# Softmax probabilities of ten units multiplied by their reciprocal on VectorE instead of GpSimd

## Chip, cores and metric

One core of a Trainium2 chip runs the whole program. The metric is the device time of one launch in microseconds (us); lower is better. The kernel before took 682.22 us (median of three runs, 682.05 to 683.24).

## What is computed

Causal attention over 4 batches, 12 heads, 448 positions and 64 columns a head, then a gated feed-forward layer on the 1792 resulting rows of 768 columns:

```python
scores = scale * np.matmul(q, k.transpose(0, 1, 3, 2))
scores = np.where(mask, -1000000000.0, scores)
attn = np.exp(scores - np.max(scores, axis=-1, keepdims=True))
attn = attn / (np.sum(attn, axis=-1, keepdims=True) + 1e-09)
attn_out = np.matmul(attn, v)
# rows x of 768 columns from attn_out, then
xn = x / np.sqrt(np.mean(x * x, axis=-1, keepdims=True) + 1e-06) * rms_g
g = xn @ w_gate
out = ((g * (1.0 / (1.0 + np.exp(-g)))) * (xn @ w_val)) @ w_out
```

The change touches one line of this: the division of `attn` by its row sums.

## The kernel before

Attention is done in **units**: two heads (`e` = 0 and 1) times a stretch of queries of one batch. The units come in three groups. The first group is units 0 to 11 (`ENDS[0]` is 12), each of 256 queries and 256 keys; its scores are held as a block of 128 queries by 128 keys and one of 128 by 256, for each of the two heads. So one step over the scores of a unit is four instructions: 128x128, 128x256, 128x128, 128x256.

What happens to one unit, engine by engine:

- TensorE makes the scores `s_ps` (line 193).
- VectorE adds the mask, scales, writes them to SBUF as `sp` and takes the row extremes `nm` (line 202, four instructions, each with a short accumulator read).
- ScalarE takes the exponential in place, with the row sums `sm` (line 205), and adds the tiny constant (line 227).
- VectorE takes the reciprocal `rs` of the four sums (`norm`, line 214).
- The probabilities `sp` are multiplied by `rs`: on GpSimd for units 0 to 9 (line 210), on ScalarE for units 10 and 11 (line 208).
- TensorE transposes `sp` into `t_ps` (head 0) and `x_ps` (head 1) (line 249). ScalarE copies the first and VectorE the second into `pt` (lines 255 and 253).
- TensorE multiplies `pt` by the values into `a_ps` (line 275), and VectorE copies that to `xr` (line 292).

Six buffers of `sp` serve three units at a time, and two banks hold `s_ps`.

The program writes every engine's order out by hand: `round_steps` gives a round of six ticks per unit, and `post(delay, fn)` puts a step some ticks later. Every engine then works through its own list in that order, and waits by semaphores alone. In the first group a round of unit p makes the scores of unit p + 3, the products of unit p, and the transposes of unit p + 1. Between these steps other work is threaded: weights are unpacked by one ScalarE step (line 414), one GpSimd step that flushes tiny values in place (line 415) and two VectorE steps (lines 417 and 419), and split into a high and a low part (lines 429 and 431); `xr` is split likewise (lines 335 and 336) and squared (GpSimd, line 103) and summed (VectorE, line 318); and the first feed-forward products run (lines 475 to 477). The GpSimd queue in this stretch holds the multiplications of line 210, the flushes of line 415 and the squares of line 103, one after the other.

After the first group the second group (products on ScalarE at line 208) and the third run threaded into the feed-forward products, and the feed-forward layer of the last rows ends the program.

Of the kernel before, what the change touches and what calls it, by code (L numbers as in the profile page):

```python
# [39 lines left out]
ENDS = [max(i for i, u in enumerate(UNITS) if u[0] == g) + 1 for g in range(NG)]  # L40
# [22 lines left out]
def attention_ffn(ctx: ExitStack, tc: tile.TileContext, qk0, qk1, qk2, v, v2, w, g, out, out2):  # L63
# [7 lines left out]
    nc = tc.nc  # L71
# [22 lines left out]
    def bank(tag, bufs=1):  # L94


        return ps.tile([P, W], F32, tag=tag, name=tag + "_ps", bufs=bufs)
# [34 lines left out]
    def post(delay, fn):  # L132
        if delay <= 0:
            fn()
        else:
            later.setdefault(now[0] + delay, []).append(fn)
# [14 lines left out]
    def load_qk(p):  # L151
        if p < len(UNITS):
            _, kind, _, _, row, _ = UNITS[p]
            raw_qk[p] = raw.tile([P, 2, W], F32, tag="qk", name="qk_r")
            if kind == 2:
                nc.sync.dma_start(out=raw_qk[p], in_=qk2[row])
            else:
                nc.sync.dma_start(out=raw_qk[p][:, 0], in_=(qk0, qk1)[kind][row])
# [10 lines left out]
    def blocks(kind):  # L169

        return [(0, P), (P, 2 * P)] if kind == 0 else [(0, KEYS[kind])]

    def steps_s(p):


        if not 0 <= p < len(UNITS):
            return []
        _, kind, _, _, _, _ = UNITS[p]
        pr = hs[p] = dict(norms=[])
        bl = blocks(kind)  # L180
        nb = 2 * len(bl)

        def scores(pss):
            for i, (o, wd) in enumerate(bl):
                for h in range(1 + (kind == 2)):
                    for e in range(2):
                        r = raw_qk[p][e * D: (e + 1) * D, h]
                        if kind == 2:
                            ps, q0, nq = pss[e][h * D: (h + 1) * D, :wd], 0, D
                        else:  # L190
                            ps, q0, nq = pss[e][:, o: o + wd], i * P, P
                        k0 = nq if kind else 2 * P
                        nc.tensor.matmul(ps, r[:, q0: q0 + nq], r[:, k0: k0 + wd],  # L193
                                         start=True, stop=True)

        def softmax(e, i, pss):
            o, wd = bl[i]
            ps, sp = pss[e][:, o: o + wd], pr["sp"][e][:, o: o + wd]
            n = len(bl) * e + i
            nm, sm, rs = (pr[m][:, n: n + 1] for m in ("nm", "sm", "rs"))  # L200
            mk = mask2 if kind == 2 else mask[:, 3 * P - wd:]
            nc.vector.tensor_tensor_reduce(  # L202
                out=sp, in0=ps, in1=mk, scale=nsc, scalar=3.0e38,
                op0=ALU.add, op1=ALU.min, accum_out=nm)
            post(T["exp" if p >= ENDS[0] else "exp0"], lambda: nc.scalar.activation(  # L205
                sp, sp, AF.Exp, bias=nm, scale=-1.0, accum_out=sm))
            if ENDS[0] - 2 <= p < ENDS[1]:
                pr["norms"].append(lambda: nc.scalar.mul(sp, sp, rs))
            else:
                pr["norms"].append(lambda: nc.gpsimd.tensor_scalar(  # L210
                    sp, sp, rs, 1.0, op0=ALU.mult, op1=ALU.mult))

        def norm():
            nc.vector.reciprocal(pr["rs"][:, :nb], pr["sm"][:, :nb])  # L214
            post(2 if ENDS[0] - 2 <= p < ENDS[0] else 0, lambda: [f() for f in pr["norms"]])

        def step():
            for nm in ("nm", "sm", "rs"):
                pr[nm] = st_p.tile([P, 4], F32, tag=nm, name=nm)
            pr["sp"] = [sp_p.tile([P, S], F32, tag="sp", name="sp") for _ in range(2)]  # L220
            pss = [bank(t_) for t_ in "xy"] if p > ENDS[1] + DP and p % 2 == 0 else [
                bank("s", 2) for _ in range(2)]
            scores(pss)
            for e in range(2):
                for i in range(len(bl)):
                    softmax(e, i, pss)
            post(T["exp" if p >= ENDS[0] else "exp0"], lambda: nc.scalar.activation(
                pr["sm"][:, :nb], pr["sm"][:, :nb], AF.Identity, bias=tiny))
            post(T["norm1" if kind else "norm0"], norm)
            post(2, lambda: load_qk(p + 4))  # L230

        return [step]
# [602 lines left out]
    with tc.manual_schedule():  # L835
# [157 lines left out]
        for q in range(21):  # L993
            i, p = divmod(q, 3)
# [58 lines left out]
```

## Time and profile before

| what | value |
|---|---|
| median of three runs | 682.22 us (682.05 to 683.24) |
| profiled execution | 681.84 us, its span 680.0 us |
| TensorE matmul busy | 667.7 us, 98% of the span |
| VectorE busy | 535.2 us, 79% |
| ScalarE busy | 378.3 us, 56% |
| GpSimd busy | 287.7 us, 42% |
| granted TensorE clock | full in every slice of the span |

The shares are means over a program of different stages. The first sixty microseconds hold the first group of units, and only they contain instructions that the change moves. In rows of the trace a line shows start and duration in us; consecutive VectorE instructions overlap at their ends, so what one of them costs the next is the distance between starts, not the duration.

### The profile page before, as it was taken

The page shows a single profiled execution, that of the slowest core. Times are in us where ns is not written, and L with a number is a line of the kernel's source. Part 1 is how long each engine was busy: PE and PEld are TensorE (multiplying, and loading weights), DVE is VectorE, ACT ScalarE, POOL GpSimd, SP SyncE. Part 2 cuts the span into 40 slices and gives each one's busy share as a digit, 9 for nine tenths or more (in the row PEclk, how much of TensorE's full clock was granted, in tenths as well). Part 3 has the DMA queues.
Part 4 walks back from the last instruction along what each step waited for, and adds up shares of the span by engine and source line. Part 5 has one row for each costly group of instructions (what it writes and reads, how often), then busy time and mean ns, then how long its engine had stood idle before and what let it go on. Part 6 is the DMA issues. An engine that isn't in the chain of part 4 may idle for free.

```text
span 680.0 us, 11926 instructions
## 1 busy us (share of the span) xinstructions
PE 667.7 (98%) x4116; PEld 550.8 (81%) x4116; DVE 535.2 (79%) x1059; ACT 378.3 (56%) x855; POOL 287.7 (42%) x262
## 2 busy tenths in 40 slices
PE   8989999999999999999999999999999999999997
PEld 5566877777777767777777777888999999999997
DVE  4998998999888486877777878487577866889982
ACT  6986779787876444545545353434534343355540
POOL 4971121222235427565765665563333342402220
PEclk9999999999999999999999999999999999999999
DMA  8765788787977556777667645316775457563541
GB/s 269 243 235 189 230 244 291 230 262 242 283 260 283 164 159 233 216 242 207 228 213 239 208 159 182 122 62 197 250 242 178 161 194 240 196 172 89 155 140 59
DMA packets 71356, 138.81 MB, mean 204 GB/s; under 512 B 7744, under 2 KB 39232, under 8 KB 71296
## 3 DMA queue, kind: packets, MB, share of 16 engines
q1 hardware_dynamic: 71296, 138.05, 63.0%
q8 instruction: 33, 0.54, 0.3%
q14 instruction: 27, 0.22, 0.1%
HBM read 104.21 MB, written 33.82 MB: 203 GB/s over the span
## 4 chain that ended last, share of the span: by engine, by line
PE 68%; DVE 1%; ACT 1%; DMA 0%; issue 0%; SPq 0%; DVEq 0%; ACTq 0%
PE s_ps L625 10%; PE m_ps L475 9%; PE m_ps L625 9%; PE m_ps L477 9%; PE m_ps L476 9%; PE y_ps L625 5%; PE a_ps L275 5%; PE x_ps L625 4%; PE t_ps L249 4%; PE s_ps L193 2%; PE x_ps L193 2%; DVE w_r L450 1%; DMA w_o<-wsum 0%; ACT sp L205 0%; ACT w_c L414 0%
## 5 line engine op out<-in xcount | busy, mean ns | idle before, releaser
L475 PE MATMUL m_ps<-xh,w_h 128*128 128x512 f32 x276 | 117.3, 425 | 0.0
L210 POOL TENSOR_SCALAR sp<-sp,rs 128x384 f32<-128x384 f32 (+2 forms) x112 | 77.7, 711 | 90.7 <-DVE rs L214 86.1
L205 ACT ACTIVATE sp<-sp,nm 128x384 f32<-128x384 f32 (+3 forms) x168 | 87.1, 521 | 41.3 <-DVE nm L202 41.3
L477 PE MATMUL m_ps<-xh,w_l 128*128 128x512 f32 x276 | 108.4, 393 | 0.0
L476 PE MATMUL m_ps<-xl,w_h 128*128 128x512 f32 x276 | 108.3, 392 | 0.0
L415 POOL TENSOR_SCALAR w<-w 128x768 f32<-128x768 f32 x36 | 39.8, 1108 | 104.4 <-ACT w_c L414 98.3
L103 POOL TENSOR_TENSOR a_l<-w_q,a_h 128x768 fp32r<-128x768 f32 x24 | 48.2, 2007 | 81.0 <-ACT a_h L516 81.0
L275 PEld LDWEIGHTS a_ps<-pt,v_r 128*64 128x64 f32 (+1 forms) x864 | 42.1, 137 | 31.9 <-issue 9.7
L275 PE MATMUL a_ps<-pt,v_r 128*64 128x128 f32 (+2 forms) x864 | 58.5, 268 | 6.0 <-DVE pt L253 3.2
L103 POOL TENSOR_TENSOR w_l<-w_r,w_h 128x768 fp32r<-128x768 f32 x30 | 59.5, 1992 | 6.2 <-ACT w_h L429 6.0
L475 PEld LDWEIGHTS m_ps<-xh,w_h 128*128 128x128 f32 x276 | 51.9, 188 | 11.8 <-issue 3.7
L477 PEld LDWEIGHTS m_ps<-xh,w_l 128*128 128x128 f32 x276 | 51.9, 188 | 11.8
L253 DVE COPY pt<-t_ps 128x384 f32<-128x384 f32 (+1 forms) x71 | 42.4, 597 | 23.9 <-PE t_ps L249 23.5
L475 PE MATMUL m_ps<-hh,w_h 128*128 128x512 f32 x144 | 58.6, 407 | 0.0
L202 DVE CUSTOM_DVE_ANT_0 sp<-s_ps,mask 128x128 f32<-128x128 f32 (+3 forms) x136 | 49.7, 414 | 10.9 <-PE s_ps L193 9.9
L476 PEld LDWEIGHTS m_ps<-xl,w_h 128*128 128x128 f32 x276 | 52.2, 189 | 7.6
L477 PE MATMUL m_ps<-hh,w_l 128*128 128x512 f32 x144 | 56.3, 391 | 0.0
L476 PE MATMUL m_ps<-hl,w_h 128*128 128x512 f32 x144 | 56.2, 390 | 0.0
L249 PE MATMUL t_ps<-ident,sp 128*128 128x128 f32 (+1 forms) x309 | 50.1, 275 | 0.1
L249 PEld LDWEIGHTS t_ps<-ident,sp 128*128 128x128 f32 (+1 forms) x309 | 37.9, 138 | 14.3 <-issue 2.0
L193 PE MATMUL s_ps<-qk_r 64*128 64x128 f32 (+3 forms) x296 | 42.6, 425 | 0.5 <-DVE nm L202 0.4
L516 ACT CAST a_h<-w_q 128x768 fp32r<-128x768 f32 (+1 forms) x48 | 35.0, 754 | 14.1 <-DMA w_q<-wz 4.3
(194 smaller groups left out, 1667.9 us busy)
## 6 DMA issues: line engine op xcount, KB each, us to landing
w<-in_w SPq DMA_DIRECT2D x36, 768.0 KB, 5.7
w<-w_c SPq DMA_DIRECT2D x36, 384.0 KB, 5.8
w_r<-w SPq DMA_DIRECT2D x36, 384.0 KB, 4.5
qk_r<-in_qk SPq DMA_DIRECT2D x48, 256.0 KB, 4.6
qk_r<-in_qk SPq DMA_DIRECT2D x12, 512.0 KB, 5.7
v_r<-in_v SPq DMA_DIRECT2D x12, 448.0 KB, 4.8
v_r<-in_v SPq DMA_DIRECT2D x24, 192.0 KB, 3.0
wy<-w_r SPq DMA_DIRECT2D x24, 192.0 KB, 4.3
```

The costliest lines, as they stand in the source:

```text
L103: nc.gpsimd.tensor_tensor(out_, a, b, op=op)
L193: nc.tensor.matmul(ps, r[:, q0: q0 + nq], r[:, k0: k0 + wd], start=True, stop=True)
L202: nc.vector.tensor_tensor_reduce(out=sp, in0=ps, in1=mk, scale=nsc, scalar=3.0e38, op0=ALU.add, op1=ALU.min, accum_out=nm)
L205: post(T["exp" if p >= ENDS[0] else "exp0"], lambda: nc.scalar.activation(sp, sp, AF.Exp, bias=nm, scale=-1.0, accum_out=sm))
L210: pr["norms"].append(lambda: nc.gpsimd.tensor_scalar(sp, sp, rs, 1.0, op0=ALU.mult, op1=ALU.mult))
L249: nc.tensor.transpose(ps[:kb, at: at + P], pr["sp"][e][:, o + kb * j: o + kb * (j + 1)], ident)
L253: nc.vector.tensor_copy(pt[:kb, :at], ps[:kb, :at])
L275: nc.tensor.matmul(av_ps[e * D: (e + 1) * D, p % 2, q0: q0 + n], raw_v[p][:kb, h, j, e, :], pr["pt", e][:kb, a0: a0 + n], start=(j == 0), ...
L475: nc.tensor.matmul(ps, wh[:, k, :], mh, start=(first and k == ks[0]), stop=False)
L476: nc.tensor.matmul(ps, wh[:, k, :], ml, start=False, stop=False)
L477: nc.tensor.matmul(ps, wl[:, k, :], mh, start=False, stop=(last and k == 5))
L625: nc.tensor.matmul(ps, a[x], b[y], start=first and n == 0, stop=last and n == 2, skip_group_check=True)
```

## The change

```diff
             if ENDS[0] - 2 <= p < ENDS[1]:
                 pr["norms"].append(lambda: nc.scalar.mul(sp, sp, rs))
+            elif p < ENDS[0]:
+                pr["norms"].append(lambda: nc.vector.tensor_scalar_mul(sp, sp, rs))
             else:
                 pr["norms"].append(lambda: nc.gpsimd.tensor_scalar(
                     sp, sp, rs, 1.0, op0=ALU.mult, op1=ALU.mult))
```

For units 0 to 9 the four multiplications of `sp` by `rs` are issued on VectorE, in the tick of the reciprocal and right behind it. Ten units give 40 instructions that leave GpSimd and 40 that VectorE gains. The orders of TensorE, ScalarE and the DMA queue are as they were. Two lines are added, so every line from 210 on has a number that is two higher in the changed kernel.

VectorE in the middle of the first group, from one reciprocal to the next scores, before:

```order
L214 RECIPROCAL rs<-sm 128x4 [waits Activation_49]
L292 COPY xr<-a_ps 128x256 [waits PE_49]
L431 TENSOR_TENSOR w_l<-w_c,w_h 128x768 [waits Activation_49]
L253 COPY pt<-x_ps 128x384 [waits PE_49]
L417 SCALAR_TENSOR_TENSOR w_287<-w_287 128x768 [waits DMAHW1_49,Pool_49]
L202 ISA sp,nm<-s_ps,mask 128x128 [waits PE_49]
```

The four multiplications stand between the reciprocal and the copy of the products now. The same place on VectorE in the changed kernel:

```order
L216 RECIPROCAL rs<-sm 128x4 [waits Activation_49]
L210 TENSOR_SCALAR sp<-sp,rs 128x128 [waits DVE_49]
L210 TENSOR_SCALAR sp<-sp,rs 128x256
L210 TENSOR_SCALAR sp<-sp,rs 128x128
L210 TENSOR_SCALAR sp<-sp,rs 128x256
L294 COPY xr<-a_ps 128x256 [waits PE_49]
L433 TENSOR_TENSOR w_l<-w_c,w_h 128x768 [waits Activation_49]
L255 COPY pt<-x_ps 128x384 [waits PE_49]
L419 SCALAR_TENSOR_TENSOR w_287<-w_287 128x768 [waits DMAHW1_49,Pool_49]
L202 ISA sp,nm<-s_ps,mask 128x128 [waits PE_49]
```

Everything behind the reciprocal, the copy of `x_ps` into `pt` among it, stands four instructions later. GpSimd at the first squares (`acc`) and the second flush (`w_287`), before:

```order
L103 TENSOR_TENSOR acc<-xr 128x512 [waits DVE_49]
L210 TENSOR_SCALAR sp<-sp,rs 128x128 [waits DVE_49,PE_49]
L210 TENSOR_SCALAR sp<-sp,rs 128x256 [waits Activation_49]
L210 TENSOR_SCALAR sp<-sp,rs 128x128 [waits PE_49,Activation_49]
L210 TENSOR_SCALAR sp<-sp,rs 128x256 [waits Activation_49]
L415 TENSOR_SCALAR w_287<-w_287 128x768 [waits DMAHW1_49]
```

And GpSimd at the same place in the changed kernel:

```order
L103 TENSOR_TENSOR acc<-xr 128x512 [waits DVE_49]
L417 TENSOR_SCALAR w_287<-w_287 128x768 [waits DMAHW1_49,Activation_49]
L103 TENSOR_TENSOR sq<-xr 128x512 [waits DVE_49]
L417 TENSOR_SCALAR w_380<-w_380 128x768 [waits DMAHW6_49,Activation_49]
```

The squares and the flushes stand directly behind one another there, each held by its own wait alone.

## Rows read from the trace of the kernel before

**Rows 1.** Windows view: stretch, length; busy us of PE, PEld, DVE, ACT, POOL:

```profile
8.70:14.80 6.10, 5.63 (x43) 3.37 (x42) 3.19 (x21) 4.91 (x19) 3.25 (x8) 1.00 0.98 346
30.00:40.00 10.00, 9.21 (x64) 6.38 (x65) 10.00 (x35) 8.67 (x28) 9.22 (x14) 1.00 0.69 236
60.00:680.00 620.00, 614.94 (x3776) 515.21 (x3776) 487.01 (x894) 329.74 (x705) 249.97 (x200) 1.00 0.63 201
```

**Rows 2.** VectorE's rows with an idle time, 14 to 50 us (timeline: start, duration):

```profile
14.83 0.18 DVE L214 RECIPROCAL rs<-sm 128x4 f32<-128x4 f32 x1 [1.48 <-ACT sm L227]
...
17.28 0.18 DVE L214 RECIPROCAL rs<-sm 128x4 f32<-128x4 f32 x1 [0.40 <-ACT sm L227]
...
20.62 0.18 DVE L214 RECIPROCAL rs<-sm 128x4 f32<-128x4 f32 x1 [0.25 <-ACT sm L227]
...
49.23 0.96 DVE L431 TENSOR_TENSOR w_l<-w_c,w_h 128x768 fp32r<-128x768 f32 x1 [0.41 <-ACT w_h L429]
```

**Rows 3.** One round of VectorE, 32.8 to 36.6 us (timeline):

```profile
32.76 0.17 DVE L214 RECIPROCAL rs<-sm 128x4 f32<-128x4 f32 x1
32.85 0.39 DVE L292 COPY xr<-a_ps 128x256 f32<-128x256 f32 x1
33.16 0.94 DVE L431 TENSOR_TENSOR w_l<-w_c,w_h 128x768 fp32r<-128x768 f32 x1
34.02 0.54 DVE L253 COPY pt<-x_ps 128x384 f32<-128x384 f32 x1
34.49 1.02 DVE L417 SCALAR_TENSOR_TENSOR w<-w 128x768 int32<-128x768 int32 x1
...
36.55 0.17 DVE L214 RECIPROCAL rs<-sm 128x4 f32<-128x4 f32 x1
```

**Rows 4.** TensorE waiting for VectorE's copy, one round and the last (timeline):

```profile
34.62 0.86 PE L275 MATMUL a_ps<-pt,v_r 128*64 128x256 f32 x6 [0.67 <-DVE pt L253]
...
47.07 0.86 PE L275 MATMUL a_ps<-pt,v_r 128*64 128x256 f32 x6 [0.29 <-DVE pt L253]
```

**Rows 5.** VectorE's only multiplication by a column before, at 59 us (timeline):

```profile
58.67 0.18 DVE L356 RECIPROCAL rc<-rc 128x4 f32<-128x4 f32 x1 [0.78 <-ACT rc L353]
58.96 0.88 DVE L358 TENSOR_SCALAR dg<-ident,rc 128x128 f32<-128x128 f32 x4
59.75 0.95 DVE L417 SCALAR_TENSOR_TENSOR w<-w 128x768 int32<-128x768 int32 x1
60.73 0.96 DVE L419 SCALAR_TENSOR_TENSOR w_c<-w_c,w 128x768 int32<-128x768 int32 x1
```

**Rows 6.** Durations of VectorE forms (groups by form; us busy, mean ns of one):

```profile
L202 DVE CUSTOM_DVE_ANT_0 sp<-s_ps,mask 128x256 f32<-128x256 f32 x48 | 19.9, 415 | 0.0
L202 DVE CUSTOM_DVE_ANT_0 sp<-s_ps,mask 128x128 f32<-128x128 f32 x48 | 13.5, 281 | 6.5 <-PE s_ps L193 6.1 <-POOL sp L210 0.4
L557 DVE SCALAR_TENSOR_TENSOR xq<-xq,g_sb,y_ps 128x384 f32<-128x384 f32 x6 | 3.7, 609 | 0.0
L761 DVE SCALAR_TENSOR_TENSOR c<-m_ps,u 128x384 f32<-128x384 f32 x4 | 2.2, 552 | 5.2 <-PE m_ps L625 5.2
```

**Rows 7.** GpSimd beside VectorE instructions that read two SBUF tensors (timelines):

```profile
31.41 0.90 POOL L415 TENSOR_SCALAR w<-w 128x768 f32<-128x768 f32 x1
31.78 1.06 DVE L318 TENSOR_TENSOR acc<-acc,sq 128x512 f32<-128x512 f32 x1
...
36.95 1.08 DVE L419 SCALAR_TENSOR_TENSOR w_c<-w_c,w 128x768 int32<-128x768 int32 x1
...
47.74 0.68 DVE L318 TENSOR_TENSOR acc<-acc,sq 128x512 f32<-128x512 f32 x1
```

**Rows 8.** A GpSimd square (timeline), and who waited for instructions with `rs` (tile view):

```profile
36.17 1.04 POOL L103 TENSOR_TENSOR sq<-xr 128x512 f32<-128x512 f32 x1
...
  PEld x_ps L249: 0.8, 3
  PEld t_ps L249: 0.7, 3
```

## Prediction

> **What bounds the kernel now.** The page comes first: TensorE is busy for 98% of the span, so only a stretch in which it stands still can give or take time. Over the last 620 us it is busy for 614.94 us [rows 1]; the edit lies ahead of them, in the first 50 us. There the windows view turns the picture round: from 30 to 40 us VectorE is busy for 10.00 us of 10.00, GpSimd for 9.22, and TensorE for only 9.21 [rows 1].
>
> Next, the timeline of VectorE alone, to see whether "busy" means that it has no slack. Between 14 and 50 us only four of its instructions have an idle time ahead of them: the reciprocals at 14.83, 17.28 and 20.62, each waiting for ScalarE's sums, and one subtraction at 49.23 [rows 2]. From 20.62 to 49.23 it works without a gap. A round there is reciprocal, copy of the products, a weight step, copy of the transposes, another step, four score steps: 32.76 to 36.55, or 3.79 us [rows 3]; other rounds hold one sum more. The last view is TensorE's waits: inside a round it waits 0.67 us for VectorE's copy `pt`, and the last such wait of the group is at 47.07 [rows 4]. So VectorE sets the length of the rounds, and TensorE takes what VectorE gives until the copy in front of 47.07.
>
> GpSimd is as full, but whoever waits for it waits little: the transposes waited 0.8 and 0.7 us in all for instructions with `rs`, those that ScalarE does for units 10 and 11 counted in [rows 8].
>
> **What the change costs, part by part.** It adds 40 instructions to the engine without slack and takes 40 from one that nearly nobody waits for.
>
> *The 128x128 multiplication.* The trace has the same instruction in another place: four multiplications of 128x128 by a column take from 58.96 to the next start at 59.75, 0.79 us or 0.20 each [rows 5].
>
> *The 128x256 multiplication* isn't in the trace. Bounds: as much as 128x128, 0.20, and 0.20 plus the 0.13 that 128 more columns cost a score step (415 against 281 ns) [rows 6], 0.33. To choose, I take the duration of the 128x128 apart. A step on 384 columns takes 552 ns with a constant and 609 with a column operand, 57 ns more [rows 6]. At 134 ns per 128 columns, 402 of the 552 are columns and 150 are fixed; with a column operand 207 are fixed. Four multiplications take 0.88 us with three steps of 0.20 between starts, so one lasts 0.28 [rows 5]; minus 207 that leaves about 75 ns for 128 columns, near half the rate of the score step. So I take 0.20 + 0.07 = 0.27.
>
> *The wait behind the reciprocal.* Before, the copy starts 0.09 us after the reciprocal's start [rows 3]. Now the next instruction reads the result. A dependent step elsewhere starts 0.03 after the end of the one it needs (59.75 + 0.95, then 60.73) [rows 5], which makes 0.20 from start to start and costs 0.11; the multiplication at 58.96 came 0.29 behind its reciprocal [rows 5], which would cost 0.20. I take 0.11; below it lies nothing at all.
>
> *Sum per unit:* 2 x 0.20 + 2 x 0.27 + 0.11 = 1.05 us, with bounds 0.80 (0.20 for all, no wait) and 1.26 (0.33 for the wide ones, 0.20 for the wait).
>
> *What of it is covered.* Units 0 and 1 are multiplied between 8.7 and 14.8 us. VectorE is busy there for 3.19 us of 6.10 [rows 1], so 2.9 idle us face 2.1 us of new work, and the reciprocal at 14.83 waits for ScalarE, which was itself held up by a weight load. I count these two units at nothing; without that cover they would cost 2.1. Unit 2 adds 1.05 behind 14.83, and the idle 0.40 at 17.28 swallows part: 0.65 late. Unit 3 adds 1.05, and the 0.25 at 20.62 goes: 1.45 late [rows 2]. Units 4 to 9 come with no idle time left: 6 x 1.05 = 6.30. The copy that TensorE waits for at 47.07 stands behind all of them: 7.75 late.
>
> *What leaves GpSimd.* Queued behind its multiplications were the flushes and squares, which now start as soon as their own inputs are there. This moves collisions with VectorE. A sum at 31.78 took 1.06 us while a flush ran from 31.41 to 32.31; the same sum with GpSimd at rest took 0.68 [rows 7]. That happens to two sums, and they would be 0.38 faster each. A weight step took 1.08 where the quiet one took 0.96 [rows 5, 7]; three of these give 0.36. Gains: 0.76 + 0.36 = 1.1. On the other side a square takes 1.04 [rows 8] and will start right behind the copy of the products. The split at 33.16 then stands ahead of it; the square runs from its end, beside the copy of the transposes, which is 0.47 from start to start (34.02 to 34.49) [rows 3], and 0.57 is left in which the next weight step finds it. The sum at 31.78 met 0.53 of a flush and lost 0.38, so 0.57 costs 0.42. Four squares: 1.7, less the four times 0.07 that the step loses today (1.02 against 0.95) [rows 3, 5], 1.4. Net +0.3, with bounds -1.1 and +1.4.
>
> The Trainium skill (SBUF — State Buffer, Who interferes with whom) has a rule for this: VectorE and GpSimd share a port pair that is an exclusive lock, for instructions with two SBUF inputs and for one-input ones in the fast mode. The row of the stretched sum agrees for two inputs; whether the new multiplications take part, no row here shows. By the rule they would, which is the second rival below.
>
> *What carries to the end.* Behind 47.07 nothing waits for a clock time: the later engines work from what TensorE, VectorE and ScalarE hand on, and TensorE has 5.1 idle us in the last 620 [rows 1]. I carry the whole delay: 7.75 + 0.3 = 8.05 us. The profiled execution took 681.84 us (span 680.0 and 1.84 around it), which makes 689.9. The median of the runs is 0.4 above that execution, so 690.3 would be as good; I keep 689.9.
>
> **The rivals.**
> 1. *The squares and flushes find gaps.* If they fall beside the score steps, the gain of 1.1 is kept and nothing is lost: 681.84 + 7.75 - 1.1 = 688.5. With the low price of 0.80 the delay is 0.40 at 17.28, 0.95 at 20.62, and 0.95 + 4.80 = 5.75 at the end, less 1.1: 686.5. For: the flushes wait for ScalarE, whose place in a round can be anywhere. Against: squares start right behind a VectorE copy.
> 2. *The lock takes the new work too.* All nine squares and flushes of the group hold up VectorE for 0.42 each, 3.8, less today's 0.3 and the gain of 1.1: 681.84 + 7.75 + 2.4 = 692.0. For: the half-rate reading of the multiplication. Against: in the rounds without a square GpSimd has nothing to do.
> 3. *Not slower: the rounds wait for the normalisation, not for VectorE.* If the chain reciprocal, GpSimd, transposes set the rounds, a shorter multiplication shortens them, by the 1.5 us of waits at most [rows 8]: 680.3. It decides if VectorE has 1.05 us of slack in a round; it has none for 28 us [rows 2]. The Trainium skill (Perfetto Trace Analysis, Optimizing GPSIMD Operations) says to prefer other engines to GpSimd where possible, which speaks for the change; the row of 10.00 us on VectorE speaks against it here.
> 4. *The delay is swallowed later.* If all 5.1 us in which TensorE stands still behind 60 us were waits for something that doesn't move, 681.84 + 8.05 - 5.1 = 684.8 would be left. Against: loads and stores are queued behind the same steps and move with them.
>
> **How the numbers follow.** Chances: forecast 0.59, rival 1 0.20, rival 2 0.12, rival 3 0.04, rival 4 0.05. The forecast's own range is 688.5 to 691.5. The low end for 8 in 10 takes in half of rival 1, 687.0; the high end is the price of 1.26 (0.86 at 17.28, 1.87 at 20.62, plus 7.56, 9.4 in all) with part of the collisions, 692.5. Beyond 0.2%, about what a measurement can tell from no change, only rival 3 at its full size is faster: 0.04. Within 0.2% are a rival 3 of no size and a rival 4 larger than I count: 0.03. The rest, 0.93, is slower.
>
> **What would show it.** In the profile after: 40 VectorE multiplications of 0.28 and 0.34 us duration, the first of each four 0.20 behind its reciprocal; rounds of about 4.8 us where one took 3.79; no VectorE idle time between about 20 and 50 us; waits of TensorE for `pt` that grow by some 6 us in all; GpSimd's busy time down by its 40 multiplications; the products of unit 9 some 8 us later; and from there every row shifted by the same amount. I am wrong if VectorE shows idle time in those rounds, if the wide multiplication takes far from 0.27, or if the shift at 60 us and the shift at the end differ.

## Result and the profile after

The changed kernel takes 688.74 us (median of four runs, 687.33 to 690.62) against 682.34 for the kernel before in the same comparison: 6.4 us more. The ratio, formed over the executions and not from the two medians, is 1.011 with an interval of 1.0091 to 1.0129, or 6.2 to 8.8 us more. The change makes the kernel slower. The forecast of 689.9 is 1.2 us above the median.

The page's first lines of the changed kernel give span and busy time of each engine:

```profile
span 688.8 us, 11879 instructions
...
PE 670.3 (97%) x4116; PEld 550.3 (80%) x4116; DVE 546.1 (79%) x1099; ACT 378.7 (55%) x855; POOL 267.6 (39%) x222
```

VectorE has 10.9 us more than the 535.2 of before and GpSimd 20.1 less than 287.7. The page doesn't tell where in the program that counts. The windows view does, here of the changed kernel, in the same three stretches as [rows 1] (the last three numbers of a line are the granted clock of TensorE, the busy share of the DMA engines and GB/s):

```profile
8.70:14.80 6.10, 5.83 (x42) 3.43 (x38) 4.50 (x25) 3.83 (x14) 0.88 (x1) 1.00 0.88 334
30.00:40.00 10.00, 7.50 (x50) 4.75 (x50) 9.93 (x36) 7.59 (x25) 2.86 (x3) 1.00 0.61 221
60.00:680.00 620.00, 616.85 (x3792) 514.28 (x3792) 494.20 (x905) 334.36 (x713) 252.29 (x202) 1.00 0.63 202
```

From 30 to 40 us VectorE is as full as before, GpSimd has gone from 9.22 busy us to 2.86, and TensorE from 9.21 to 7.50. The relieved engine rests and the one that TensorE depends on does less for it in the same ten microseconds. From 8.7 to 14.8 us VectorE had room: 4.50 busy us where there were 3.19.

One round of VectorE in the changed kernel (timeline: start, duration; it answers to [rows 3]):

```profile
37.98 0.17 DVE L216 RECIPROCAL rs<-sm 128x4 f32<-128x4 f32 x1
38.18 1.01 DVE L210 TENSOR_SCALAR sp<-sp,rs 128x128 f32<-128x128 f32 x4
39.10 0.42 DVE L294 COPY xr<-a_ps 128x256 f32<-128x256 f32 x1
39.44 0.95 DVE L433 TENSOR_TENSOR w_l<-w_c,w_h 128x768 fp32r<-128x768 f32 x1
40.30 0.55 DVE L255 COPY pt<-x_ps 128x384 f32<-128x384 f32 x1
40.77 1.33 DVE L419 SCALAR_TENSOR_TENSOR w<-w 128x768 int32<-128x768 int32 x1
...
43.13 0.17 DVE L216 RECIPROCAL rs<-sm 128x4 f32<-128x4 f32 x1
```

The round takes 5.15 us where it took 3.79. The row of four multiplications starts 0.20 behind the reciprocal, and the copy starts 1.12 behind it, where it was 0.09. The weight step of line 419 took 1.33 where the same step took 1.02 [rows 3], beside GpSimd's square, which now runs from 39.67 on; without the square it takes 0.94 (a run below). Timeline of GpSimd, changed kernel:

```profile
29.29 1.68 POOL L103 TENSOR_TENSOR sq<-xr 128x512 f32<-128x512 f32 x1 [6.53 <-DVE xr L294]
30.94 1.59 POOL L417 TENSOR_SCALAR w<-w 128x768 f32<-128x768 f32 x1
39.67 1.62 POOL L103 TENSOR_TENSOR sq<-xr 128x512 f32<-128x512 f32 x1 [7.14 <-DVE xr L294]
41.26 1.61 POOL L417 TENSOR_SCALAR w<-w 128x768 f32<-128x768 f32 x1
```

The square waits for VectorE's copy of the products at 39.10, and its 1.62 us against 1.04 in [rows 8] show that GpSimd is held up too, here beside VectorE's split of 39.44. TensorE's waits inside a round and behind the last one (timeline, changed kernel) answer to [rows 4]:

```profile
40.91 0.86 PE L277 MATMUL a_ps<-pt,v_r 128*64 128x256 f32 x6 [0.67 <-DVE pt L255]
...
55.31 0.86 PE L277 MATMUL a_ps<-pt,v_r 128*64 128x256 f32 x6 [0.45 <-DVE pt L255]
```

The last stood at 47.07 and stands at 55.31, 8.24 us later.

### The profile page after: what moved, and what is told of

The parts are those of the page before. It is cut to its first block, busy times and chain, and to the rows that moved or that the text cites. A ratio compares the mean times of both kernels' runs of the same rounds, so it can differ in the third digit from the quotient of the medians.

```text
span 688.8 us, 11879 instructions
## 1 busy us (share of the span) xinstructions
PE 670.3 (97%) x4116; PEld 550.3 (80%) x4116; DVE 546.1 (79%) x1099; ACT 378.7 (55%) x855; POOL 267.6 (39%) x222
## 4 chain that ended last, share of the span: by engine, by line
PE 62%; DVE 3%; DMA 2%; issue 1%; ACT 1%; SPq 0%; DVEq 0%; ACTq 0%
PE m_ps L477 9%; PE m_ps L479 8%; PE m_ps L478 8%; PE s_ps L627 8%; PE m_ps L627 7%; PE a_ps L277 5%; PE y_ps L627 4%; PE t_ps L251 4%; PE x_ps L627 4%; PE s_ps L193 2%; PE x_ps L193 2%; DVE a_l L520 1%; DMA w_o<-w 1%; DMA out_t<-ob 1%; DVE w_r L452 1%
## 5 line engine op out<-in xcount | busy, mean ns | idle before, releaser
L417 POOL TENSOR_SCALAR w<-w 128x768 f32<-128x768 f32 x36 | 41.4, 1151 | 117.3 <-ACT w_c L416 112.6
L212 POOL TENSOR_SCALAR sp<-sp,rs 128x384 f32<-128x384 f32 (+1 forms) x72 | 53.8, 765 | 80.0 <-DVE rs L216 69.6
L277 PE MATMUL a_ps<-pt,v_r 128*64 128x128 f32 (+2 forms) x864 | 61.2, 268 | 11.2 <-DVE pt L255 4.9
```

Of the source, the lines that this page charges most:

```text
L212: pr["norms"].append(lambda: nc.gpsimd.tensor_scalar(sp, sp, rs, 1.0, op0=ALU.mult, op1=ALU.mult))
L277: nc.tensor.matmul(av_ps[e * D: (e + 1) * D, p % 2, q0: q0 + n], raw_v[p][:kb, h, j, e, :], pr["pt", e][:kb, a0: a0 + n], start=(j == 0), ...
```

## Experiments

A time called "more" or "less" below is the difference of two medians; the ratio and its interval are formed over the executions. The measure beside the time is the distance between reciprocals, which needs no common start. The trace of before has 5.79 us from the reciprocal of unit 2 to that of unit 4 (14.83 to 20.62) and 24.45 from there to that of unit 10 (45.07). The changed kernel has 7.63 (15.45 to 23.08) and 30.37 (to 53.45): 1.84 and 5.92 more.

**The theory** was that VectorE has no slack from unit 2 on, so that each unit costs the 1.05 us of its four multiplications, and that collisions with GpSimd add little. **The rivals** were that the lock takes the multiplications too, that the rounds wait for the normalisation, and that something later swallows the shift.

### Half of the units, then the other half

Units 0 to 3 alone:

```diff
-            elif p < ENDS[0]:
+            elif p < 4:
```

> Only units 0 to 3 are multiplied on VectorE, units 4 to 9 on GpSimd as before. If the cost is VectorE time in the stretch where it has no idle time (the theory): units 0 and 1 cost nothing, units 2 and 3 leave 1.45 us, so 1.0 to 2.0 us over the kernel before. If every unit cost the same share of what the changed kernel lost (6.4 us over ten units): 2.6 us. If the lost time came from TensorE at half clock around 17 to 21 us: most of the loss is here already, 3 us or more.

Measured: 684.98 against 681.39, ratio 1.0041 (1.0022 to 1.006), 3.6 us more by the medians and 2.8 by the ratio (1.5 to 4.1). That is above the 1.0 to 2.0 of the theory, and by the time alone the equal shares (2.6) fit as well. The trace decides: units 2 to 4 take 7.56 us, 1.77 more than before, and the six units behind take 24.45 as before; the granted clock is full in all windows from 10 to 30 us. The rest lies behind the rounds, where TensorE's clock falls in this execution (shown in the section on the clock). Seven of the twelve executions had a mean granted clock of 0.997 and took 684.5 us on average; the seventeen executions of the kernel before with that mean, over all comparisons, took 682.4. At equal clock 2.1 us are left.

Units 4 to 9 alone:

```diff
-            elif p < ENDS[0]:
+            elif 4 <= p < ENDS[0]:
```

> Only units 4 to 9 are multiplied on VectorE, units 0 to 3 on GpSimd as before. The theory: 6 x 1.05 = 6.3 us, with collisions of three squares 6 to 7 us over the kernel before, and no low clock at 17 to 21 us. Equal shares: 3.8 us. Low clock as the cause: under 4 us.

Measured: 687.73 against 681.39, ratio 1.0084 (1.0061 to 1.0107), 6.3 us more. Units 4 to 10 take 31.01 us, 6.56 more. It is 0.64 above the whole change there, all of it in the first round, in which a flush that GpSimd does behind the multiplications of unit 3 meets the four of VectorE (timelines of this run):

```profile
21.19 1.64 DVE L210 TENSOR_SCALAR sp<-sp,rs 128x128 f32<-128x128 f32 x4
...
21.30 0.94 POOL L417 TENSOR_SCALAR w<-w 128x768 f32<-128x768 f32 x1
```

1.64 us against 1.01 with GpSimd at rest is a first sign that the multiplications take part in the contention. The two halves show where the time is: nearly 2 us in units 2 and 3, some 6 in units 4 to 9.

### The work added, none removed

The kernel before, with the same 40 multiplications on VectorE in addition, written into a mask that is filled only later (the lines that move this fill, a GpSimd step, behind the first group are left out here):

```diff
+            if p < ENDS[0] - 2:
+                for n in range(4):
+                    o, wd = bl[n % 2]
+                    nc.vector.tensor_scalar_mul(
+                        mask2[:, o: o + wd], mask[:, o: o + wd], pr["rs"][:, n: n + 1])
```

> The kernel before keeps its multiplications on GpSimd; VectorE gets 40 multiplications of the same two shapes behind the same ten reciprocals, which write to a tile that nobody reads until later (the second mask, built later). It computes the same result and does the multiplications in addition. The theory: VectorE's time is what costs, so it is as slow as the changed kernel or up to 2 us slower, 6.5 to 9 us over the kernel before. If taking the work off GpSimd had given something back in the changed kernel, this one is slower than that by what it gave (1.1 us by my sum). If the new wait of the transposes for VectorE were the cause, this one is no slower than 1 us over before.

Measured: 694.67 against 681.39, ratio 1.0192 (1.0168 to 1.0215), 13 us more, well above the 6.5 to 9 that were expected. Units 2 to 4 take 8.38 us, 2.59 more, and units 4 to 10 34.17, 9.72 more, or 1.62 a unit. The timelines of VectorE and GpSimd in this run:

```profile
40.85 0.17 DVE L216 RECIPROCAL rs<-sm 128x4 f32<-128x4 f32 x1
41.05 1.34 DVE L220 TENSOR_SCALAR mask<-mask,rs 128x128 f32<-128x128 f32 x4
42.31 0.41 DVE L301 COPY xr<-a_ps 128x256 f32<-128x256 f32 x1
42.65 1.16 DVE L440 TENSOR_TENSOR w_l<-w_c,w_h 128x768 fp32r<-128x768 f32 x1
...
41.18 1.82 POOL L212 TENSOR_SCALAR sp<-sp,rs 128x128 f32<-128x128 f32 x4 [2.49 <-DVE rs L216]
42.97 1.73 POOL L103 TENSOR_TENSOR sq<-xr 128x512 f32<-128x512 f32 x1
```

Both engines start their four multiplications at the same reciprocal and hold each other up: from start to start VectorE needs 1.26 us for four where 0.92 was enough in the changed kernel, and GpSimd 1.82 where it took 1.62 at 15.10 in the kernel before. The step behind takes 1.16 instead of 0.95. So the work added costs 1.62 a unit and the work removed gives about 0.6 back. The change is worth the difference, near 1.0. The new wait of the transposes for VectorE isn't what costs, since here they still wait for GpSimd. The forecast put that gain in the flushes and squares only. The Trainium skill (SBUF — State Buffer, Who interferes with whom) lets instructions with one SBUF input take part in the lock when they run in their fast mode; the 1.34 here and the 1.64 above agree, and settle what the prediction had left open.

### Half of the four multiplications

Only the two blocks of 128x128 on VectorE, the two of 128x256 on GpSimd:

```diff
-            elif p < ENDS[0]:
+            elif p < ENDS[0] and i == 0:
```

> Units 0 to 9 with the two 128x128 blocks on VectorE and the two 128x256 blocks on GpSimd. If the prices add up as in the sum (2 x 0.20 and 0.11 for the wait, against 1.05 for all four), the delay is 0.51 a unit, units 4 to 10 take 24.45 + 3.1 = 27.5 us and the time is about 3 us above before. If the multiplications on the two engines hold each other up as in the run that kept both, each unit costs 0.2 to 0.3 more, units 4 to 10 take 28.7 to 29.3 us and the time is 4.5 to 5 us above before. If VectorE hides half of the work, under 1.5 us.

Measured: 686.68 against 681.62, ratio 1.0074 (1.005 to 1.0097), 5.1 us more. Units 4 to 10 take 29.05 us (20.77 to 49.82), 0.77 a unit: the second theory, with a time at the upper end of it. Timelines of this run:

```profile
35.09 0.16 DVE L216 RECIPROCAL rs<-sm 128x4 f32<-128x4 f32 x1
35.29 0.71 DVE L210 TENSOR_SCALAR sp<-sp,rs 128x128 f32<-128x128 f32 x2
35.92 0.41 DVE L294 COPY xr<-a_ps 128x256 f32<-128x256 f32 x1
...
35.44 0.93 POOL L212 TENSOR_SCALAR sp<-sp,rs 128x256 f32<-128x256 f32 x2 [2.53 <-ACT w_c L416]
```

Two small multiplications take 0.63 from start to start beside GpSimd's, where four take 0.20 each with GpSimd at rest [rows 5]. Half of the instructions, with a third of the columns, cost three quarters of what the whole change costs in these rounds (4.6 of 5.92).

### Does VectorE set the rounds, or GpSimd?

The kernel before without three of the four sums of squares (columns 1 to 3), which leaves out that part of the norm of the rows. It takes work from VectorE and nothing from the chain reciprocal, GpSimd, transposes:

```diff
-            elif c < NP - 1:
+            elif NP - 3 < c < NP - 1:
```

> The kernel before without three of its VectorE sums of squares (line 318, for the columns 1 to 3), so it leaves out a part of the first group's row norms. Two of the three stand in the stretch without idle time and take 0.98 us each from start to start. If VectorE sets the rounds: 1.5 to 2.5 us faster than before, with unit 10's reciprocal 1.9 us earlier. If the rounds wait for the chain through GpSimd's multiplication: no change beyond 0.5 us, and VectorE idle for about 0.98 us in those rounds instead.

Measured: 679.59 against 681.37, ratio 0.9974 (0.9962 to 0.9986), 1.8 us less, inside what was expected. Units 4 to 10 take 22.67 us, 1.78 less, and VectorE still has no idle time between 21.41 and 46.99. Of the 1.96 us that VectorE is spared in these rounds they give back 1.78; the rest is in two weight steps, which take 1.11 where they took 1.02. The rival by which the rounds wait for GpSimd falls.

### Squares out of the way

The changed kernel with the four squares replaced by a fill with ones, so that the norms of the rows are left out of the result:

```diff
-                pool_op(sq, x, ALU.mult, x)
+                nc.gpsimd.memset(sq, 1.0)
```

> The changed kernel with GpSimd's four squares of the first group replaced by a fill with ones of the same tile, which reads nothing (so the first group's row norms are not the reference's). If the weight step of 1.33 us (0.95 when quiet) is held up by GpSimd's reading of SBUF: those steps go to 0.95, the rounds with them are 0.3 to 0.4 us shorter, four in all, 1.2 to 1.6 us faster than the changed kernel. If any GpSimd instruction holds VectorE up, or the flush does it: no difference beyond 0.5 us.

Measured: 690.18 against 681.37, ratio 1.0128 (1.011 to 1.0147), 1.4 and 2.3 us above the two medians of the changed kernel (688.74 and 687.9). Neither theory had it slower. Units 4 to 10 take 31.11 us, 0.75 more than there. The weight step does take 0.94 (at 30.96) instead of 1.33, as expected, but the flush, no longer queued behind a square, starts earlier and meets something else (timelines of VectorE and GpSimd in this run):

```profile
29.21 1.36 DVE L433 TENSOR_TENSOR w_l<-w_c,w_h 128x768 fp32r<-128x768 f32 x1
...
38.31 1.74 DVE L210 TENSOR_SCALAR sp<-sp,rs 128x128 f32<-128x128 f32 x4
...
38.24 0.53 POOL L314 MEMSET sq<- 128x512 f32 x1 [8.47 <-DVE acc L320]
38.73 0.98 POOL L417 TENSOR_SCALAR w<-w 128x768 f32<-128x768 f32 x1
```

The split takes 1.36 instead of 0.95, the multiplications 1.74 instead of 1.01. Taking a collision away moved it.

### VectorE relieved by as much as it was given

The changed kernel with VectorE's part of the split (line 433) of the first four weights on GpSimd:

```diff
-            if s < NU or s > NU + 2 * NF and s % 2:
+            if 3 < s < NU or s > NU + 2 * NF and s % 2:
```

> The changed kernel with the low-part subtraction of the first four weights (line 433) on GpSimd, which stands idle there. It takes 0.87 us from start to start off VectorE in every second round, three times in the stretch without idle time. If only VectorE's own instruction times count: 2.6 us faster than the changed kernel. If the port that both engines use counts as much: GpSimd's subtraction (about 2 us on this size) holds up VectorE's multiplications or weight steps, and less than 1 us is left of it.

Measured: 687.97 against 681.37, ratio 1.0097 (1.0082 to 1.0113), the time of the changed kernel, so the second theory. Units 4 to 10 take 29.87 us, 0.5 less, although three splits of 0.87 each have left that stretch. VectorE still has no idle time between 14.21 and 56.60; the time went into its other steps. Two sums of squares took 1.22 and 1.21 where they were 0.69 and 0.68, three weight steps 1.55 to 1.62 where they were 1.33, and one group of four multiplications 1.25 where it took 1.01 (timelines of this run):

```profile
26.53 1.25 DVE L210 TENSOR_SCALAR sp<-sp,rs 128x128 f32<-128x128 f32 x4
...
35.65 1.22 DVE L320 TENSOR_TENSOR acc<-acc,sq 128x512 f32<-128x512 f32 x1
...
38.71 1.62 DVE L419 SCALAR_TENSOR_TENSOR w<-w 128x768 int32<-128x768 int32 x1
...
25.12 1.86 POOL L103 TENSOR_TENSOR w_l<-w_c,w_h 128x768 fp32r<-128x768 f32 x1 [3.64 <-ACT w_h L431]
```

### The clock in the first trace of the changed kernel

In the profiled execution TensorE stood still for 2.39 us ahead of 17.10, and the windows view then shows a granted clock below full (columns as in [rows 1]):

```profile
18.00:20.00 2.00, 2.00 (x9) 1.38 (x7) 1.97 (x12) 0.31 (x1) 0.00 (x0) 0.50 0.31 114
20.00:22.00 2.00, 2.00 (x14) 1.27 (x14) 1.71 (x4) 2.00 (x7) 1.88 (x2) 0.70 0.04 8
```

0.50 is the level of 1.2 GHz. VectorE felt it: its copy of the transposes waited 0.29 us for TensorE, which it does not in the second trace of the changed kernel (timelines of VectorE, the first trace, then the second):

```profile
20.33 0.56 DVE L255 COPY pt<-x_ps 128x384 f32<-128x384 f32 x1 [0.29 <-PE x_ps L251]
20.80 1.17 DVE L419 SCALAR_TENSOR_TENSOR w<-w 128x768 int32<-128x768 int32 x1
...
20.12 0.55 DVE L255 COPY pt<-x_ps 128x384 f32<-128x384 f32 x1
20.59 1.56 DVE L419 SCALAR_TENSOR_TENSOR w<-w 128x768 int32<-128x768 int32 x1
```

Whether this costs time was tested twice. With TensorE kept busy by eight products that nobody uses:

```diff
+            if done == 25:
+                warm(8)
```

> The changed kernel, with eight 128x128 matmuls of ones (their result is read by nobody) in TensorE's queue between the scores of unit 4 and the products of unit 1, where the changed kernel's TensorE stood still for 2.4 us and then ran at half clock until 21 us. If VectorE alone sets the time: within 0.5 us of the changed kernel (688.7), though the clock stays full. If the low clock costs what lies between the changed kernel's fastest and slowest runs (687.3 to 690.6): about 687.3, with runs within 1 us of each other.

Measured: 689.04 against 681.39, ratio 1.0107 (1.0084 to 1.013). The time is within 0.5 us of 688.74, as expected if VectorE alone sets it. The granted clock is full in all stretches from 10 to 30 us, and units 2 to 4 and 4 to 10 take 7.56 and 30.37 us. And the changed kernel once more:

> The changed kernel once more, unaltered. By the walk over the rounds the delay is 7.75 us plus 0.3 of collisions; the runs so far gave 6.4 over the kernel before. Expected 6 to 8.5 us over before, and in its trace unit 10's reciprocal 7.5 to 9 us later than in the kernel before.

Measured: 687.9 against 681.37, ratio 1.0097 (1.0083 to 1.0111). This is 6.5 us over before, and unit 10's reciprocal comes 8.2 to 8.5 us later than in the two traces of before, both as expected. This execution shows no dip, and 7.56 and 30.36 us. In the first trace, in which ScalarE waited 2.16 us for a weight ahead of the standstill, the copy comes 1.84 us behind the reciprocal of 18.49, in the second 1.46 behind that of 18.66. But the weight step behind it waits for GpSimd's square and ends 0.81 us behind the square's end (21.16 and 21.34) in both traces, so the scores start 3.41 us behind the reciprocal in both. Units 2 to 4 take 7.63 and 7.56 us. So the dip cost 0.07 us at most, in part by luck: a collision stood behind it and took up the delay.

Where VectorE does not set the pace, the same level costs time. In the run with units 0 to 3 alone the granted clock is 0.50 from 62 to 64 us, behind the first group, although TensorE was busy for 1.87 of the 2.00 us from 58 to 60. The windows view of that run:

```profile
60.00:70.00 10.00, 10.00 (x43) 7.22 (x44) 7.66 (x14) 4.32 (x6) 0.00 (x0) 0.83 0.48 159
```

From the first of the products that sum the squares over columns to the first product of the closing part this execution takes 422.76 us (57.84 to 480.60). Both traces of the kernel before take 421.57, those of the changed kernel 421.66 and 421.60. Of the twelve traces four show such a spell at half clock between 55 and 80 us and take 422.6 to 422.8; the other eight take 420.6 to 421.8.

### The kernel before once more

> The kernel before once more, for a second trace of it. The executions with the change end their last part (from the first product of the closing feed-forward stretch to the end) in 201.7 to 203.6 us; the one trace of before took 203.2 there. If that is a spread of executions, this run shows some other value between 201.5 and 204.5 for the same code, its time is within 1 us of the median of before, and its reciprocals of units 4 and 10 are 24.4 to 24.5 us apart as in the first trace. If the tail belonged to the kernel, it shows 203.2 again and the shift of 8.8 us seen in the first pair of traces stands against medians that say 6.5.

Measured: 681.58 against 681.62, ratio 0.9997 (0.9976 to 1.0019). Units 4 to 10 take 24.46 us. The stretch behind the first product of the closing part is 201.99 us here where it was 203.15 in the first trace, for the same code. So single executions differ by about 1 us in that part, and the end of one pair of traces is no measure of the shift. The same product of the closing part, in the first trace of before and of after, then in the second of each (timelines):

```profile
476.85 0.34 PE L625 MATMUL m_ps<-ch,a_h 128*128 128x384 f32 x1
485.19 0.34 PE L627 MATMUL m_ps<-ch,a_h 128*128 128x384 f32 x1
477.11 0.34 PE L625 MATMUL m_ps<-ch,a_h 128*128 128x384 f32 x1
485.23 0.34 PE L627 MATMUL m_ps<-ch,a_h 128*128 128x384 f32 x1
```

It comes 8.34 and 8.12 us later. The spans are 680.0 and 688.8 in the first pair, 679.1 and 686.9 in the second: 8.8 and 7.8 more.

## Why the prediction was right

**The bound.** VectorE has no idle time in the changed kernel between 20.33 and 57.32 us, and the runs say that it sets the rounds. Less work for it in the kernel before shortened them by 1.78 of the 1.96 us taken off, more work lengthened them by more than its own price (9.72 for 6 x 1.05), and in the one trace with TensorE at half clock they were no longer than 0.07 us. Only where the work went to GpSimd instead did 0.5 of 2.6 us come back: what counts is VectorE's time with its hold-ups, not its list alone.

**The price of a unit.** The groups by form of VectorE in the first 60 us of the changed kernel (us busy, mean ns of one):

```profile
L210 DVE TENSOR_SCALAR sp<-sp,rs 128x256 f32<-128x256 f32 x20 | 7.0, 348 | 0.0
...
L210 DVE TENSOR_SCALAR sp<-sp,rs 128x128 f32<-128x128 f32 x20 | 5.7, 284 | 0.4
```

Durations of 0.34 and 0.28 were predicted, as was the start 0.20 behind the reciprocal. Reciprocal to copy has gone from 0.09 to 1.13 (27.66 to 28.79): 1.04 a unit, where the sum had 1.05. The reading of the wide multiplication at half the rate of the score step, chosen between 0.20 and 0.33, was the right one.

**Units 0 and 1** were counted at nothing. The reciprocal of unit 2 is at 14.21 to 15.62 in the runs of the changed kernel and its variants that have these two units on VectorE, and at 14.83, 15.04, 15.20 and 15.61 in the four where GpSimd does them. No cost can be seen beside what the weight loads do from one execution to the next. In the two traces in which units 0 and 1 have their reciprocals at the same times (9.35 and 12.50), the run without sums and the second one of the changed kernel, unit 2 has its at 15.61 and 15.62.

**Units 2 and 3** were put at 1.45, and cost 1.77 to 1.84. The rest is the first square's collision, which was counted with the others: the step of line 419 took 1.56 us in the second trace of the changed kernel, where the second trace of before has 1.11 (0.42 was put on a square). In the first trace it took 1.17, with VectorE's wait for TensorE ahead of it.

**Units 4 to 9** were put at 6.30 and 0.3 for collisions, and cost 5.92. Six times 1.04 is 6.24. Three weight steps of 1.33, where they took 1.11, 1.02 and 1.02, add 0.84. Two sums of 0.69 and 0.68, where they took 1.06 [rows 7], give back 0.75 (0.76 predicted). The quieter steps of lines 421 and 338 give 0.48 (0.36 predicted, for the first of them alone). The sum is 5.85. So the collisions give back near 0.4 in this stretch and take about as much in the one before; the forecast had 0.3 on the side of loss. The size of one collision was foretold well: the square that ends at 30.97 meets the weight step of 30.45 for 0.52 us and costs it 0.38, where 0.57 and 0.42 were predicted. Over both stretches 7.7 to 7.8 us stand against 8.05; that the first was put too low and the second too high, so that half of the miss cancels, is luck.

**The carry.** The products of unit 9 come 8.24 us later, the products that sum the squares over columns 8.25 (55.28 to 63.53), the closing part 8.1 to 8.3. Nothing up to there swallows it, and the rival of 684.8 falls. Some 0.6 us of the 8.24 stand ahead of unit 2 already, whose reciprocal comes at 15.45 where it came at 14.83 (15.62 and 15.04 in the second pair): the start differs from one execution to the next. The medians differ by 6.4 and 6.5 us, the one with the added products by 7.65, and the rounds by 7.7. Single executions of the kernel before range from 679.06 to 683.5 us in ten runs, and part of that goes with the clock: of its 57 executions with a clock on record the eighteen with a mean granted clock of 1.000 took 680.6 us on average, the seventeen with 0.997 682.4. At a mean of 1.000 the changed kernel took 688.0 (three executions), 7.4 us more, and at 0.999 687.8 against 681.15 (three and nineteen), 6.65 more. No run tested this part, and the gap of up to 1 us that is left stays open.

**The lock** (second rival) was given the right mechanism and the wrong result. The multiplications do take part in it. Yet in the changed kernel none of the forty is held up, each group of four lasts 1.01 us in both traces: GpSimd has 2.86 us of 10 left, and its squares and flushes run behind VectorE's copy of the products and end before the next reciprocal. They meet weight steps, not multiplications.

**Two signs were wrong.** TensorE's waits for `pt` were to grow by some 6 us. In the first 70 us they grew from 2.7 to 4.5 us; beside them stand 4.3 under `sp`, 2.39 of it the single standstill ahead of 17.10, and 1.2 under `xr`, two names under which nothing stood before. In the second pair of traces it is 3.2 and 4.5, 3.0 and 0.6. Without the standstill these waits have grown by 4.9 us in either pair. The name under which TensorE waits depends on which of several late things comes last. And the round of 3.79 us was to take about 4.8: it takes 5.15, because the sign left out the square's collision that the sum had counted (3.79 + 1.05 + 0.35).

## What to carry to other kernels

Before work is moved from a full-looking engine, find which of the full engines has no idle time ahead of its instructions and who waits for it: here GpSimd was 92% busy and harmless, VectorE 100% busy and the bound. A busy share can hold time in which the engine is held up (below). Price the moved instructions from the same form elsewhere in the trace, start to start, with the wait that the new place gives them. Where two engines hold each other up, half of the work moved can cost nearly as much as all of it: 0.77 us a unit here against 0.99.

## What was not expected of the hardware

- Multiplying an SBUF block by a column is held up on VectorE by what GpSimd does at the same time: four take 0.92 us from start to start alone and 1.26 beside the same four on GpSimd; two small ones take 0.63 instead of 0.40 beside GpSimd's two wide ones.
- It works in both directions. GpSimd's flush of 768 columns took 0.90 us in the middle of its own queue [rows 7] and 1.59 to 1.62 in the changed kernel, where it meets VectorE's steps; three of its four squares 1.61 to 1.68 instead of 1.04. With VectorE's split moved away the squares took 1.04 again (28.20 in that run). By these rows the split holds up the square, the square the weight step, and the weight step the flush.
- The engine that was relieved had been held up itself. In the kernel before the smaller block took GpSimd longer than the larger one, by groups by form (us busy, mean ns of one):

```profile
L210 POOL TENSOR_SCALAR sp<-sp,rs 128x128 f32<-128x128 f32 x20 | 15.9, 797 | 10.7 <-DVE rs L214 10.7
...
L210 POOL TENSOR_SCALAR sp<-sp,rs 128x256 f32<-128x256 f32 x20 | 9.5, 475 | 0.0
```

The quickest 128x128 took 0.37 us, and four multiplications 1.62 us from 15.10 on, beside VectorE's copies and scores, but 3.12 from 33.09 on, beside its split and weight step [rows 3]. So part of the 9.22 busy us of GpSimd in [rows 1] was waiting, and it cost the kernel nothing.

- Such collisions are hard to take out one by one: with the squares gone the time rose by 1.4 to 2.3 us, and with a step moved away it stayed as it was, because GpSimd's next instruction took their place.
